# First layer of six experts as seven block products: a fused RWKV and top-1 expert kernel on one Trainium2 core

## The chip, the cores and the metric

The kernel runs on one core of a Trainium2 chip. The core has five engines with a queue of instructions each: TensorE (PE: matmuls; its weight loads are listed apart as PEld), VectorE (DVE), ScalarE (ACT), GpSimd (POOL) and SyncE (SP, which starts transfers here). They run side by side and meet only at semaphores; each takes its own instructions in order. TensorE writes to PSUM, which has eight banks of 512 fp32 numbers on each of 128 partitions; the other operands lie in SBUF. The metric is device time in microseconds for one execution; lower is better.

## The reference

All is fp32. Four sequences of 768 tokens with 8 heads of 48 go through a linear recurrence; its output, 3072 tokens of 384 numbers, goes to a layer of eight experts, of which each token visits the one with the highest logit:

```python
for t in range(S):
    cur = np.einsum('bhd,bhe->bhde', u[None] * kt, vt)
    y[:, :, t] = np.einsum('bhd,bhde->bhe', rt, state + cur)
    state = w[None, :, :, None] * state + np.einsum('bhd,bhe->bhde', kt, vt)
...
expert_idx = np.argmax(logits, axis=1)
gate_w = probs[np.arange(N), expert_idx]
for e in range(E):
    mask = expert_idx == e
    h = np.maximum(x[mask] @ w1[e], 0.0)      # 384 x 1024
    out[mask] = gate_w[mask, None] * (h @ w2[e])   # 1024 x 384
```

## The kernel before

**Order of the work.** Everything stands in an order written out by hand; each engine runs its part of that order, and waits between engines are put in where a tile is written and read (or written again). First comes the recurrence, 16 pairs of heads in chunks of 128 tokens (TensorE lines L276 to L349, with VectorE's scale L257, GpSimd's products L263 and L267, and `turn`, a GpSimd copy of one element, which holds GpSimd back until a certain tile is written). Each token's row is then written to a table in memory, sorted by expert. Two `early` passes take the first 160 tokens of experts 0 and 1. Then eight `late` passes follow, `k` = 0 to 7: 0 and 1 take the rest of experts 0 and 1, 2 to 7 take the other six experts by falling number of tokens. Their widths `n` are 224, 192, 416, 412, 408, 396, 380 and 364 columns (`WIDTH`, L35); a token is a column. A column beyond an expert's count is padding and isn't written out.

**A pass.** `load` brings the tokens (SP's queue), `xT` transposes them on VectorE (L457) into `t`, three tiles `m` of 128 numbers by `n` tokens. `L1` (L460) is the first layer: for each of eight tiles `f` of 128 hidden numbers, three matmuls over `m` into one of four banks (`hbank`, L70), and ScalarE's Relu (L468) out of the bank into `h`. The 1024 hidden numbers come in four quarters of two tiles, one weight tile `w1s[k % 2][q]` each. `L2` (L473) is the second layer for the columns beyond the first 256 (`c`): 24 products into three banks (`ybank`, L71), transposed back by VectorE (L482), weighted (L493) and scattered to the output by GpSimd (L499, L606). `tokens_out` (L501) is the second layer for the first 256 tokens of passes 2 to 7, in a 2x2x2 block form that is there already: two blocks of tokens, of hidden numbers and of output columns, seven products of blocks (L526) instead of eight. It needs sums of blocks of the weights (`weight_sums`, L579: eight operations on VectorE into `tums`) and of `h` (`inner_sums`, L594: four on VectorE into `sums`). VectorE and ScalarE combine its products (L544 to L559), and GpSimd scatters the rows of two blocks of 128 tokens (L573, L577).

**How the passes interleave** (L793 to L826). In pass `k` < 7 TensorE runs the first layer of pass `k` and then the second layer (`L2`, `tokens_out`) of pass `k - 1`, called `o`. Between the two, in VectorE's order, stand `o`'s sums and the transposes of pass `k + 1`. Then the loads of later weights and tokens are started. In the last stage `o`'s second layer comes ahead of pass 7's first layer, and pass 7's second layer ends the kernel. For `k` < 3 the output blocks of the early passes are scattered between the tiles of the first layer (L800 to L802).

**PSUM.** `X01[0]` and `X01[1]` are tiles of one bank. `X23` (L63) is one tile of two banks, used as `X23[:, 0, :]` and `X23[:, 1, :]`. `yps[0]`, `yps[1]`, `dsb` and `tr` are tiles of one bank each. The first layer uses the X banks, the second layer the others.

**A guard.** A flag counts conditions that the sorted form rests on; if one fails, a general program runs instead. One is a least number of tokens of each sorted expert (`lows`, L643).

Of the kernel before, what the change touches and what calls it, by code (L numbers as in the profile page):

```python
# [26 lines left out]
FT = F // 128  # L27
# [16 lines left out]
def straight(tc, rk, vk, w, w1, w2, out, flag):  # L44
# [26 lines left out]
    ybank = [yps[0], dsb, yps[1]]  # L71

# [357 lines left out]
    class Pass:  # L430
# [29 lines left out]
        def L1(self, fs=range(FT), then=()):  # L460

            h, then = self.h, list(then)
            for f in fs:
                p = hbank[f % 4]
                for m in range(DT):
                    nc.tensor.matmul(p[:, 0:self.n], lhsT=w1s[self.k % 2][f // 2][:, m, f % 2 * 128:(f % 2 + 1) * 128],  # L466
                                     rhs=self.t[:, m, 0:self.n], start=m == 0, stop=m == DT - 1, skip_group_check=True)
                nc.scalar.activation(h[:, f, 0:self.n], p[:, 0:self.n], func=ACT.Relu)  # L468
                if then:
                    load, k, q = then.pop(0)  # L470
                    load(k, (q,), nc.scalar)

        def L2(self):  # L473
# [3 lines left out]
            for m in range(DT):  # L477
                p = ybank[m]
# [22 lines left out]
        def tokens_out(self):  # L501
# [66 lines left out]
            product(dsb, 0, Sm(2), Tm(2))  # L568
            product(dsb, 1, Sm(3), B_(1, 1))
            add(so[6], dsb, 0, so[2])  # L570
            final(1, 1, dsb, 0, so[5])
            final(0, 1, dsb, 1, so[4])
            scatter(out, it2[:, 0:1], self.yt[0][:, :], N)  # L573
            weigh(so[7], so[6], 1)
            product(yps[1], 0, A(1, 1), Tm(3))
            final(1, 0, yps[1], 0, so[7])
            scatter(out, it2[:, 1:2], self.yt[1][:, :], N)  # L577

        def weight_sums(self):  # L579
# [5 lines left out]
            for q in range(2):  # L585
                o = slice(2 * q, 2 * q + 2)
                (b11, b12), (b21, b22) = [[halves(ws[q + u])[:, :, z] for z in range(2)] for u in (0, 2)]
                t1, t2, t3, t4 = [x[:, o].rearrange("p f (m c) -> p f m c", m=DT) for x in tums]
                op(t1, b12, b11, ALU.subtract)
                op(t2, b22, t1, ALU.subtract)  # L590
                op(t3, b22, b12, ALU.subtract)
                op(t4, b21, t2, ALU.subtract)

        def inner_sums(self):  # L594
# [5 lines left out]
            op(sums[0], a21, a22, ALU.add)  # L600
            op(sums[1], sums[0], a11, ALU.subtract)
            op(sums[2], a11, a21, ALU.subtract)
            op(sums[3], a12, sums[1], ALU.subtract)
# [11 lines left out]
    def op(o, a, b, how):  # L615
        nc.vector.tensor_tensor(o, a, b, op=how)
# [26 lines left out]
    nc.gpsimd.memset(lows[:, 2:], 256.0)  # L643
# [112 lines left out]
    so = [mp.tile([128, DM // 2], FP32, name=f"so{k}") for k in range(8)]  # L756
    vt, ia = [mp.tile([128, nt], I32, name=n) for n in ("vt", "ia")]
# [33 lines left out]
    waiting = [(x, j) for x in early for j in range(ge)]  # L791

    for k, p in enumerate(late):  # L793
        o = late[k - 1]
        if k < n - 1:

            for f in range(FT):
                p.L1((f,))
                if (k < 2 and f % 2 or k == 2 and f % 4 == 1) and waiting:
                    nc.gpsimd.tensor_copy(turn, p.h[0:1, f, 0:1])  # L800
                    x, j = waiting.pop(0)
                    x.blocks_out((j,))  # L802
            if k > 0:
                o.weight_sums()
                o.inner_sums()
            late[k + 1].xT()
            if k == 0:
                okay()
# [5 lines left out]
        else:  # L814
            o.weight_sums()
            o.inner_sums()
            o.L2()
            o.tokens_out()
            p.weight_sums()
            p.L1()  # L820
            weights1(p.k + 2)
            p.inner_sums()
# [519 lines left out]
```

## Time and profile before

| | |
|---|---|
| median of 9 runs | 386.67 us (384.38 to 389.01) |
| the profiled execution | 385.27 us |
| its span in the profile | 383.5 us |
| TensorE busy, matmuls | 367.9 us, 96% |
| VectorE, ScalarE, GpSimd busy | 48%, 35%, 40% |
| granted TensorE clock | 0.993 |
| first layer (L466), early and late | 384 + 96 matmul instructions |
| GpSimd's scatters of output (L606) | 57 |

The profile's page gives each engine's busy time, the chain of work that ended last (followed back from the last instruction to what released it each time), and groups of instructions: line, engine, operation, output from inputs, shape and number, then busy time and the mean duration of one, then the idle time in front of them and who ended it. The trace behind it can be asked for single instructions in order of time: start, duration, what. A product in fp32 is two matmul instructions for TensorE, so a first layer of 24 products is 48 instructions. Mean durations of matmuls overlap; what one adds to the row is read from how far apart they start, or from the chain.

### The profile page before, as it was taken

Reading aid. Unit: us, or ns where it says so; the run is one execution under the profiler, and the core shown is the slowest. Engines: PE = TensorE matmul, PEld = TensorE weight load, DVE = VectorE, ACT = ScalarE, POOL = GpSimd, SP = SyncE. Lnnn points to the kernel's source line nnn. Section 1 sums busy time; section 2 is a strip of 40 time slices with the busy share of each in tenths; the row PEclk is TensorE's granted clock in tenths of the full one; section 3 lists DMA queues with packets and bytes.
Section 4 is the critical chain, followed back from the end, with each engine's and each line's share of the span. In section 5 each row is a group of like instructions: output and inputs, shape, how many; then the busy total and the mean of one; then the engine's idle time right before and its main releaser. Section 6 shows DMA issues by size and latency. Waiting matters only on the chain.

```text
span 383.5 us, 8205 instructions
## 1 busy us (share of the span) xinstructions
PE 367.9 (96%) x3141; PEld 302.5 (79%) x3141; DVE 183.6 (48%) x437; ACT 133.4 (35%) x378; POOL 151.8 (40%) x176
## 2 busy tenths in 40 slices
PE   6999999999999999999999999999999999999990
PEld 6788888888877989995585599579669769996790
DVE  8977796895961224022115323702813722564331
ACT  2678787786773310310211202211220221112110
POOL 3379678888753420544113005105203402542042
PEclk9999999999999999999999999999999999999997
DMA  7998886867464883696728615823833833403301
GB/s 208 266 260 235 256 258 218 265 213 237 153 178 159 256 314 65 201 244 191 168 89 234 155 45 163 222 84 103 228 108 118 201 127 123 129 34 103 109 20 48
DMA packets 34977, 65.03 MB, mean 170 GB/s; under 512 B 18378, under 2 KB 19410, under 8 KB 34928
## 3 DMA queue, kind: packets, MB, share of 16 engines
q1 hardware_dynamic: 29392, 49.86, 46.7%
q0 software_dynamic: 3808, 9.84, 7.2%
q10 hardware_dynamic: 1728, 4.72, 3.6%
q8 instruction: 26, 0.43, 0.5%
q14 instruction: 23, 0.19, 0.1%
HBM read 53.29 MB, written 11.26 MB: 168 GB/s over the span
## 4 chain that ended last, share of the span: by engine, by line
PE 89%; issue 4%; POOL 2%; DVE 2%; ACT 1%; DMA 0%; DVEq 0%; ACTq 0%; POOLq 0%
PE X L466 33%; PE yps L480 10%; PE X L288 6%; PE yps L526 6%; PE yps L331 5%; PE dsb L480 5%; PE tr L526 4%; PE tr L349 4%; PE dsb L526 3%; PE yps L336 3%; PE tr L513 3%; PE dsb L311 2%; PE X L349 2%; PE dsb L276 2%; ACT A L294 1%
## 5 line engine op out<-in xcount | busy, mean ns | idle before, releaser
L466 PE MATMUL X<-xT,w1s 128*128 128x224 f32 (+7 forms) x384 | 113.9, 457 | 0.0
L466 PEld LDWEIGHTS X<-xT,w1s 128*128 128x128 f32 x384 | 71.4, 190 | 40.0 <-issue 21.2
L606 POOL DMA_INDIRECT out_dram<-yo,ix x33 | 32.3, 980 | 126.0 <-DVE ia L507 118.4
L468 ACT ACTIVATE hT<-X 128x224 f32<-128x224 f32 (+7 forms) x64 | 29.6, 462 | 118.4 <-PE X L466 101.9
L294 ACT ACTIVATE A<-ident,own 128x128 f32<-128x128 f32 x192 | 57.9, 388 | 8.2 <-DVE own L280 6.3
L401 POOL DMA_INDIRECT rows<-xb,slot x24 | 28.1, 1169 | 14.9 <-issue 10.1
L480 PEld LDWEIGHTS yps<-hT,w2s 128*128 128x128 f32 x256 | 32.5, 191 | 1.7 <-issue 0.9
L480 PE MATMUL yps<-hT,w2s 128*128 128x96 f32 (+7 forms) x256 | 33.3, 283 | 0.0
L288 PE MATMUL X<-RK 48*128 48x128 f32 x384 | 30.3, 289 | 1.8 <-DVE RK L257 1.8
L482 DVE STREAM_TRANSPOSE yq<-yps 128x160 f32<-128x160 f32 (+3 forms) x16 | 5.1, 318 | 52.5 <-PE yps L480 51.7
L288 PEld LDWEIGHTS X<-RK 48*128 48x128 f32 x384 | 24.0, 187 | 7.5 <-issue 4.3
L257 DVE TENSOR_TENSOR RK<-rk,TT 112x1536 f32<-112x1536 f32 x16 | 27.7, 1732 | 0.0
L263 POOL TENSOR_TENSOR rp<-rk 112x768 f32<-112x768 f32 x15 | 27.3, 1820 | 0.0
L300 DVE COPY_PREDICATED A<-strict,X 128x512 f32<-128x512 int32 x32 | 23.1, 738 | 4.5 <-ACT A L294 4.4
L331 PE MATMUL yps<-A,vk 128*48 128x128 f32 x384 | 24.3, 276 | 0.0
L606 POOL DMA_INDIRECT out_dram<-yt,it x14 | 15.4, 1101 | 20.8 <-ACT so L555 12.1
L331 PEld LDWEIGHTS yps<-A,vk 128*48 128x48 f32 x384 | 20.2, 123 | 1.9
L457 DVE STREAM_TRANSPOSE xT<-xs 128x416 f32<-128x416 f32 (+3 forms) x24 | 11.3, 521 | 20.8 <-DMA xs<-rows 20.8
L672 POOL COPY turn<-own 1x1 f32<-1x1 f32 x14 | 16.7, 1193 | 9.7 <-DVE own L280 9.2
L349 PE MATMUL tr<-sel,yT 112*128 112x104 f32 x128 | 18.6, 286 | 0.3 <-issue 0.3
L559 ACT COPY so<-tr 128x192 f32<-128x192 f32 x6 | 1.9, 320 | 48.2 <-PE tr L526 48.2
L349 PEld LDWEIGHTS tr<-sel,yT 112*128 112x128 f32 x128 | 15.7, 191 | 2.5 <-issue 0.4
(160 smaller groups left out, 529.3 us busy)
## 6 DMA issues: line engine op xcount, KB each, us to landing
w1s<-in_w_dram SPq DMA_DIRECT2D x36, 384.0 KB
rk<-in_rk_dram SPq DMA_DIRECT2D x16, 672.0 KB
w2s<-in_w_dram SPq DMA_DIRECT2D x24, 384.0 KB
vk<-in_vk_dram SPq DMA_DIRECT2D x16, 528.0 KB
w2s<-in_w_dram ACTq DMA_DIRECT2D x8, 384.0 KB
xs<-rows SPq DMA_DIRECT2D x16, 169.0 KB
w1s<-in_w_dram ACTq DMA_DIRECT2D x4, 384.0 KB
rows<-zt SPq DMA_DIRECT2D x1, 1248.0 KB
```

Of the source, the lines that this page charges most:

```text
L257: nc.vector.tensor_tensor(RKs[i % 3][0:KP].rearrange("p u (c t) -> p u c t", t=C), x[0:KP].rearrange("p u (c t) -> p u c t", t=C), bc(TT[: ...
L263: (eng or nc.gpsimd).tensor_tensor(rps[i % 2][0:KP], x[0:KP, 0], x[0:KP, 1], op=ALU.mult)
L288: nc.tensor.matmul(o, lhsT=r[q, 1, c * C:(c + 1) * C], rhs=r[q, 0, c * C:(c + 1) * C], start=True, stop=True, skip_group_check=True)
L294: nc.scalar.activation(A[:, place(c, h), :], ident, func=ACT.Copy, scale=own[i % 2][:, c, h:h + 1])
L331: nc.tensor.matmul(o(c, h), lhsT=v[:, c, h * D:(h + 1) * D], rhs=A[:, place(c, h), :], start=c < 2, stop=c == 0, skip_group_check=True)
L349: nc.tensor.matmul(trv[c // 4][:, c % 4, :], lhsT=yTs[i % 3][0:KP, c & 1, (c // 2) * C:(c // 2 + 1) * C], rhs=sel[:, c & 1, i % HP, :], st ...
L401: s_ = nc.gpsimd.indirect_dma_start(out=rows[:, :], out_offset=bass.IndirectOffsetOnAxis(ap=slot[b % 2][:, c:c + 1], axis=0), in_=xbs[b % ...
L466: nc.tensor.matmul(p[:, 0:self.n], lhsT=w1s[self.k % 2][f // 2][:, m, f % 2 * 128:(f % 2 + 1) * 128], rhs=self.t[:, m, 0:self.n], start=m ...
L468: nc.scalar.activation(h[:, f, 0:self.n], p[:, 0:self.n], func=ACT.Relu)
L480: nc.tensor.matmul(p[:, 0:n], lhsT=w2s[self.k % 2][f // 2][:, f % 2, m * 128:(m + 1) * 128], rhs=self.h[:, f, self.c:self.n], start=f == 0 ...
L526: nc.tensor.matmul(p[:, at * Z:(at + 1) * Z], lhsT=a(f), rhs=b(f), start=f == 0, stop=f == FT // 2 - 1, skip_group_check=True)
L606: s_ = nc.gpsimd.indirect_dma_start(out=to[:, :], out_offset=bass.IndirectOffsetOnAxis(ap=at, axis=0), in_=x, in_offset=None, bounds_check ...
```

## The change

The first layer of passes 2 to 7 takes the 2x2x2 block form as well, one quarter at a time (in pass 7 the first three quarters; the fourth stays as it was). The blocks are tiles `m` = 0 and 1, the two hidden tiles of the quarter, and two halves of the tokens; tile `m` = 2 is added to the same four outputs by plain products, one of them joined with another through `S[4]`. That makes 11 products of n/2 columns for 12 half products of each kind before. `quarter` gives their order and the banks: `pa` to `pd` are four banks, one set (`quads`) for quarters 0 and 2, the other for 1 and 3. VectorE and ScalarE combine the products into `h`.

The products need sums of weight blocks (`quarter_sums`: five VectorE operations of 128 by 128 a quarter, done a pass ahead) and of token blocks (`token_sums`: four of 128 by n/2 a pass). The late `L2` moves to the X banks (`zbank`). `weight_sums` of the second layer goes from VectorE to GpSimd. `inner_sums` is split into four, one behind each quarter. `tokens_out` computes its fifth and sixth product in the other order, in banks of their own, and issues its first scatter before the last two products. The guard's least number of tokens rises from 256 to 320.

```diff
+    zbank = hbank[0::2] + [X23[:, 0, :]]
+    quads = [zbank + [X23[:, 1, :]], [yps[0], dsb, yps[1], tr]]
...
+        def quarter(self, q):
+            n, w, t, sd = self.n // 2, w1s[self.k % 2][q], self.t, quart[q]
+            pa, pb, pc, pd = quads[q % 2]
+            def W(m, f):
+                return w[:, m, f * 128:(f + 1) * 128]
+            def T(m, z):
+                return t[:, m, z * n:(z + 1) * n]
+            def product(p, at, *ab):
+                for j, (a, b) in enumerate(ab):
+                    nc.tensor.matmul(p[:, at * n:(at + 1) * n], lhsT=a, rhs=b, start=j == 0, stop=j == len(ab) - 1,
+                                     skip_group_check=True)
+            def both(p):
+                return p[:, 0:2 * n].rearrange("p (z j) -> p z j", z=2)
+            S = [sd[:, j, :] for j in range(5)]
+            Y = [toks[j][:, 0:n] for j in range(4)]
+            a, u, v, x = mids[q % 2]
+            product(pa, 0, (W(0, 0), T(0, 0)))
+            product(pb, 0, (W(1, 0), T(1, 0)), (W(2, 0), T(2, 0)))
+            nc.scalar.copy(a[:, 0:n], pa[:, 0:n])
+            product(pb, 1, (S[1], Y[1]))
+            nc.vector.tensor_tensor(u[:, 0:2, 0:n], both(pb), bc(a[:, None, 0:n], [128, 2, n]), op=ALU.add)
+            product(pa, 1, (S[0], Y[0]), (W(2, 1), T(2, 1)))
+            nc.vector.tensor_tensor(v[:, 0:n], pa[:, n:2 * n], u[:, 1, 0:n], op=ALU.add)
+            product(pc, 1, (S[2], Y[2]))
+            product(pc, 0, (S[3], T(1, 1)), (S[4], T(2, 1)))
+            f = slice(2 * q, 2 * q + 2)
+            second = self.h[:, f, n:2 * n]
+            nc.vector.tensor_tensor(second, both(pc), bc(v[:, None, 0:n], [128, 2, n]), op=ALU.add)
+            nc.scalar.activation(second, second, func=ACT.Relu)
+            nc.vector.tensor_tensor(x[:, 0:n], pc[:, n:2 * n], u[:, 1, 0:n], op=ALU.add)
+            product(pd, 0, (W(1, 1), Y[3]), (W(2, 1), T(2, 0)))
+            nc.vector.tensor_tensor(u[:, 2, 0:n], pd[:, 0:n], x[:, 0:n], op=ALU.add)
+            nc.scalar.activation(self.h[:, f, 0:n], u[:, 0:3:2, 0:n], func=ACT.Relu)
+        def quarter_sums(self, q):
+            w, sd = w1s[self.k % 2][q], quart[q]
+            a11, a21 = [w[:, 0, f * 128:(f + 1) * 128] for f in range(2)]
+            a12, a22 = [w[:, 1, f * 128:(f + 1) * 128] for f in range(2)]
+            op(sd[:, 0, :], a21, a22, ALU.add)
+            op(sd[:, 1, :], sd[:, 0, :], a11, ALU.subtract)
+            op(sd[:, 2, :], a11, a21, ALU.subtract)
+            op(sd[:, 3, :], a12, sd[:, 1, :], ALU.subtract)
+            op(sd[:, 4, :], w[:, 2, 0:128], w[:, 2, 128:256], ALU.subtract)
+        def token_sums(self):
+            n = self.n // 2
+            b11, b12, b21, b22 = [self.t[:, m, z * n:(z + 1) * n] for m in range(2) for z in range(2)]
+            y = [toks[j][:, 0:n] for j in range(4)]
+            op(y[0], b12, b11, ALU.subtract)
...
-                p = ybank[m]
+                p = (zbank if self.nt else ybank)[m]
...
-            product(dsb, 0, Sm(2), Tm(2))
-            product(dsb, 1, Sm(3), B_(1, 1))
-            add(so[6], dsb, 0, so[2])
-            final(1, 1, dsb, 0, so[5])
-            final(0, 1, dsb, 1, so[4])
+            product(dsb, 0, Sm(3), B_(1, 1))
+            final(0, 1, dsb, 0, so[4])
             scatter(out, it2[:, 0:1], self.yt[0][:, :], N)
+            product(yps[1], 0, Sm(2), Tm(2))
+            add(so[6], yps[1], 0, so[2])
             weigh(so[7], so[6], 1)
-            product(yps[1], 0, A(1, 1), Tm(3))
-            final(1, 0, yps[1], 0, so[7])
+            final(1, 1, yps[1], 0, so[5])
+            product(tr, 0, A(1, 1), Tm(3))
+            final(1, 0, tr, 0, so[7])
...
-                op(t1, b12, b11, ALU.subtract)
+                op(t1, b12, b11, ALU.subtract, nc.gpsimd)
...
-    nc.gpsimd.memset(lows[:, 2:], 256.0)
+    nc.gpsimd.memset(lows[:, 2:], float(PAD))
...
+        if k == n - 1:
+            o.weight_sums()
+            o.inner_sums()
+            o.L2()
+            o.tokens_out()
+            p.weight_sums()
+            for q in range(3):
+                p.quarter(q)
+            p.L1(range(6, FT), bank=quads[1][2:] + quads[1][:2])
...
+                o.weight_sums()
+                for q in range(4):
+                    p.quarter(q)
+                    o.inner_sums((q,))
+                    if q > 1:
+                        late[k + 1].quarter_sums(q - 2)
...
             late[k + 1].xT()
+            if ahead:
+                late[k + 1].token_sums()
+                for q in range(0 if k == 1 else 2, 4 if k < n - 2 else 3):
+                    late[k + 1].quarter_sums(q)
```

## The prediction

> **What bounds the kernel now.** I read the page's first part, then the chain that ended last, then the groups of instructions by shape, then the order of single instructions on VectorE, ScalarE and GpSimd.
>
> ```profile
> PE 367.9 (96%) x3141; PEld 302.5 (79%) x3141; DVE 183.6 (48%) x437; ACT 133.4 (35%) x378; POOL 151.8 (40%) x176
> ```
>
> ```profile
> 178.23 16.76 PE X L466 x48
> 194.99 1.73 PE yps L480 x16
> ...
> 222.11 2.17 PE yps L480 x16
> 224.28 2.17 PE dsb L480 x16
> ...
> 228.63 2.60 PE tr L526 x16
> ...
> 300.89 15.32 PE X L466 x48
> ```
>
> From 149.9 us on, every piece of the chain is TensorE and each starts where the one before ends: TensorE has no gap in the expert part, so this part is as long as TensorE's instructions. Anything that shortens them shortens the kernel, and any wait put on TensorE lengthens it by its full length. The other engines are busy less than half the time; they matter only where TensorE is made to wait for them.
>
> ```profile
> L466 PE MATMUL X<-xT,w1s 128*128 128x416 f32 x48 | 16.9, 512 | 0.0
> ...
> L526 PE MATMUL dsb<-tums,sums 128*128 128x192 f32 x48 | 8.8, 326 | 0.0
> ...
> L616 DVE TENSOR_TENSOR tums<-w2s,w2s 128x384 f32<-128x384 f32 x12 | 6.6, 551 | 0.0
> ...
> L482 DVE STREAM_TRANSPOSE yq<-yps 128x160 f32<-128x160 f32 x8 | 2.8, 350 | 40.1 <-PE yps L480 40.1
> ...
> L263 POOL TENSOR_TENSOR rp<-rk 112x768 f32<-112x768 f32 x15 | 27.3, 1820 | 0.0
> ...
> L267 POOL TENSOR_TENSOR Kd<-vk,T 128x480 f32<-128x480 f32 x11 | 13.2, 1202 | 0.0
> ```
>
> Prices. By the chain, 48 matmul instructions (each fp32 product is two) of 416 columns take 16.76 us, 349.2 ns each, and 16 of 192 columns 2.60 us, 162.5 ns: 2.5 ns and 0.833 ns a column. VectorE's two-operand operation takes 152 ns and 1.04 ns an element (384: 0.55, 480: 0.65 us); one that needs nothing of its forerunner starts 0.08 us before that ends. GpSimd's takes 172 ns and 2.15 ns an element, so 1.0 us at 384.
>
> **Part 1: fewer columns.** A quarter had 12 instructions of n columns; it has 11 products of n/2, 22 instructions. A pass goes from 48 at n to 88 at n/2. For n = 416: 88 x 175.8 ns = 15.47 us for 16.76, 1.29 less; 412, 408, 396, 380: 1.27, 1.26, 1.22, 1.17 less. The last pass changes three quarters: 66 x 154.2 ns + 12 x 305.8 ns = 13.85 for 14.68, 0.83 less. Sum: **-7.04 us**, all on the path. That is sure: the rows of 192 columns run at that price in an unbroken row.
>
> **Part 2: the wait inside every even quarter.** The changed program's instruction order with its waits shows what the diff doesn't. In quarters 0 and 2 blocks pc and pd are the two halves of one tile, X23. The program keeps them apart as one tile: the first product of pd (toks3 into X23, second bank) waits for VectorE's `x` operation, which reads pc, the first bank. In quarters 1 and 3 the four blocks are four tiles, and that product waits for nothing. pd is the last block of a quarter, and TensorE takes its instructions in order, so the next quarter stands behind it. `x` itself comes after `second`, and `second` needs the last product of pc. So TensorE issues pc's last product, then stands idle for:
> - 0.16 us until that product is out (the group of L480 that starts at 221.94 ends at 224.28, and the next one starts at 224.12);
> - 0.04 until VectorE starts (224.28 to the transpose at 224.32);
> - `second`, 416 elements, 0.585 less 0.08: 0.50;
> - `x`, 208 elements: 0.37 (192: 0.36);
> - 0.05 back to TensorE (at the start of the attention, VectorE's L257 ends at 9.28 and TensorE's L288 starts at 9.33);
> - restart of TensorE, not shown apart in the trace: 0 (L288's weight load and matmul both start at 9.33) to 0.19 (one weight load); I take 0.05, nearest to that row.
>
> That is 1.17 us at n = 416 and 1.09 at 364, on average 1.14. There are two such quarters in each of six passes: 12 x 1.14 = **+13.7 us**. Bounds: without the first 0.16 (matmul ends are modelled) and the restart 12 x 0.93 = 11.2; with a full weight load each 15.4.
>
> **Part 3: the wait for the copy of pa.** The second half of pa likewise waits for ScalarE's copy `a` of its first half (same tile). That copy stands on ScalarE behind the Relu of the quarter before, which needs VectorE's last operation of that quarter. From the end of pd: 0.20 to VectorE, 0.37 for it, 0.05, Relu 0.52 less 0.10 overlap, copy 0.34 (192: 0.32), 0.05: 1.43 us. TensorE has four products in front, 1.41 us at n = 416 and 1.23 at 364. So quarters 1 and 3 wait 0.02 to 0.20, with the restart about 0.1, 11 times: 1.1. In front of quarter 2 the odd quarter's own `second` and `x` push VectorE's last operation back by 0.2: about 0.35, six times: 2.1. **+3.2 us**; bounds 0.5 (latencies a tenth shorter) and 6.
>
> **Part 4: weight sums on GpSimd.** Eight operations of 384 elements leave VectorE (0.55 each, 4.4 us a pass) and cost GpSimd 8.0 us. In passes 3 to 6 they stand behind the two token scatters of the pass before and end some 11 us into the pass; TensorE first reads them after its first layer, L480's products and the first two of L526, 23 us or more in: nothing, and the scatters queued behind them become ready only after that as well. In the last stage only the 5.4 us of L480 and two products of 1.30 stand between. GpSimd starts there some 2 us late (its scatters), six of the eight must be done, and the inner sums share its operands' way (below): ready at 9 to 10 us, wanted at 8.6: **+1.2 us**, bounds 0 and 4.
>
> **VectorE, queues, tail.** In the pass from 205.51 to 237.73 VectorE is busy 12.4 us. It gets 4 x 2.2 us of combining, 20 operations of 128 elements (0.23 apart, 4.6) and 4 of n/2 (1.4), and loses 4.4: near 23 us of a pass of 34. A quarter needs 2.2 us of it, with an inner sum (0.6) and the next pass's weight sums (1.15) 4.0, while TensorE takes 3.9 plus the waits; the two sets of four banks give a quarter's slack, so its load alone costs nothing. For pass 2 the transposed tokens (1.6), token sums (1.4) and weight sums (4.6) run from 167.11, where the tokens land, and with the second layer's transposes behind them end near 176.5; TensorE wants them at 178.23: 1.7 us spare. The loads on SP's queue wait for the same last readers as now, with a pass to land in: nothing. The tail: the first token scatter is ready two products earlier: -0.3.
>
> Sum against the profiled execution (385.27 us, span 383.5): -7.0 + 13.7 + 3.2 + 1.2 - 0.3 = +10.8, so 396.1. That execution lies 1.4 under the median of the runs, 386.67; from there **397.4 us**, 2.8% slower.
>
> **A rule weighed.** VectorE and GpSimd get in each other's way in this trace:
>
> ```profile
> 41.48 1.72 DVE L257 TENSOR_TENSOR RK<-rk,TT 112x1536 f32<-112x1536 f32 x1
> 41.69 1.55 POOL L672 COPY turn<-own 1x1 f32<-1x1 f32 x1 [1.28 <-DVE own L280]
> ...
> 62.96 2.12 POOL L672 COPY turn<-own 1x1 f32<-1x1 f32 x1 [0.36 <-issue]
> ...
> 15.75 1.19 POOL L267 TENSOR_TENSOR Kd<-vk,T 128x480 f32<-128x480 f32 x1
> 16.72 1.84 DVE L257 TENSOR_TENSOR RK<-rk,TT 112x1536 f32<-112x1536 f32 x1
> ```
>
> A copy of one element, 0.18 us elsewhere, takes 1.55 and ends when VectorE's L257 ends; the other way round L257 takes 1.84 instead of 1.72 where it starts inside a GpSimd operation. The Trainium skill, "SBUF — State Buffer", section "Who interferes with whom", says that a VectorE instruction with two SBUF inputs and a GpSimd instruction that reads SBUF exclude each other for a whole instruction. The rows agree, and it speaks against moving the weight sums: the inner sums (two SBUF inputs) now run beside them. By that rule, with turns taken, an inner sum waits for at most one GpSimd operation, which the quarter's slack holds, and the sum stays at 397.4; without any exclusion the last stage would wait 0.3 instead of 1.2 and the sum be 396.5.
>
> **The rivals.**
> 1. *GpSimd keeps the way for its whole run.* The copy at 62.96 (2.12 us) waits out two VectorE operations that follow each other without a gap, so a run may hold on. Then the inner sum after quarter 0 waits up to four operations, and with it VectorE, ScalarE's copy and quarter 2: some 1.3 us in each of passes 3 to 6: +5.5, 402.9. Against it: four of eight operations wait for the one before, which leaves gaps.
> 2. *The waits cost their lower bounds:* -7.3 + 11.2 + 0.5 = +4.4, 391.1.
> 3. *Other side: the wait for `x` is met before TensorE arrives,* and the saved columns remain: 386.67 - 7.0 - 0.3 + 1.2 = 380.6. It decides once the idle time of an even quarter is under 7.3 / 12 = 0.6 us. `second` and `x` alone stream 624 elements, 0.65 us at 1.04 ns. Hardly.
> 4. *The change does not do what it says.* The order has 88 matmul instructions for 48 and the sums on GpSimd; only the price could differ. Busy time over count gives 8.8 / 48 = 183 ns for 192 columns; at that price 88 of 208 columns (196 ns) take 17.3 us against 16.76 and the columns cost 2.9 us instead of saving 7.0: 407. But each group's busy time holds the 0.16 us in which it overlaps the next, and the chain's 162.5 ns doesn't.
>
> **Chances.** Forecast 0.68, rival 1 0.20, rival 2 0.07, rival 3 and any other gain 0.05. The range, 391.5 to 404, takes in both ends of the waits and rival 1; the forecast's own is 393 to 401. About 0.5% can be told from no change here: faster 0.05, same 0.03, slower 0.92.
>
> **What would show it.** In the changed profile: matmul groups of 208 columns near 15.4 us of issue a pass; idle time of TensorE before the X23 products of the first layer, released by VectorE's `x` line, 12 times near 1.1 us, and none before those of tr; short idle times before pa's second half, released by ScalarE's copy; one wait for GpSimd in the last stage; a TensorE share below 96%. No idle time before X23 would make the forecast wrong; idle times of several microseconds released by the copy in passes 3 to 6 would be rival 1.

## The result, and the profile after

The changed kernel takes **409.0 us** (median of 10 runs, 407.4 to 412.2) against 387.29 for the kernel before beside it: 1.0565 times as long, 95% interval 1.0531 to 1.0598. The forecast of 397.4 had the sign and half of the size, and the time lies outside its range. The profiled execution has a span of 406.4 us (383.5 before).

The experiments ran in five more sessions on five chips, and the six sessions fell into two kinds. The kernel before takes 385 to 387 us in the one and 381 in the other; the changed kernel tells them apart much more clearly:

| | before, us | changed, us | ratio (95%) |
|---|---|---|---|
| first comparison | 387.29 | 409.0 | 1.0565 (1.0531 to 1.0598) |
| again, in another session | 385.83 | 407.25 | 1.0551 (1.0485 to 1.0616) |
| again, in a third one | 380.82 | 393.38 | 1.0311 (1.0279 to 1.0343) |

I call the chip of the first two "late" (the reason comes below; whether it was one chip or two isn't known) and that of the third "prompt". On the prompt one the change costs 12.6 us, near the 10.7 forecast; on the late ones some 9 us more. Since each of the five chips was met in one session only, "chip" here and below can also mean the occasion.

The page's first part, of the changed kernel on a late chip and then on the prompt one:

```profile
PE 371.1 (91%) x3371; PEld 336.1 (83%) x3371; DVE 244.8 (60%) x643; ACT 140.2 (34%) x401; POOL 201.7 (50%) x224
```

```profile
PE 366.2 (93%) x3371; PEld 333.8 (85%) x3371; DVE 246.5 (63%) x643; ACT 140.3 (36%) x401; POOL 201.9 (52%) x224
```

TensorE's share fell from 96% by waits. They are these: TensorE's waits from 150 us on (line, what it waited for, us in total, times, longest), late chip, then prompt chip (from 140 us):

```profile
PE X L490 <- DVE midx L512: 11.7, 12, 1.3
PE X L490 <- ACT mida L501: 6.3, 9, 1.7
PE yps L591 <- POOL tums L680: 2.4, 1, 2.4
```

```profile
PE X L490 <- DVE midx L512: 11.2, 12, 1.0
PE X L490 <- ACT mida L501: 1.0, 5, 0.2
PE yps L591 <- POOL tums L680: 0.6, 1, 0.6
```

The first row is the wait for `x`, twelve times, as forecast, on both kinds. The second and third rows differ by 5.3 and 1.8 us. The view counts idle time from the end of the matmul before, which otherwise overlaps the next one by 0.16 us, so each wait costs 0.16 us more than it says. The first matmul behind a wait costs another 0.10 us (0.28 from its start to the next one, where 0.17 to 0.18 is usual), and waits under some 0.15 us are not in the view.

Where it lies, in lengths of the first layer (from its first matmul to the next layer's first) and of the stretch of second layers ahead of pass 7:

| us | pass 2 | 3 | 4 | 5 | 6 | 7 | last stage's second layers |
|---|---|---|---|---|---|---|---|
| before (both profiles, late chips) | 16.8 | 16.6 | 16.4 | 16.0 | 15.3 | 14.7 | 29.3 to 29.5 |
| changed, prompt chip | 18.8 | 18.6 | 18.4 | 17.9 | 17.3 | 16.9 | 30.2 |
| changed, late chip (first) | 18.9 | 18.6 | 20.2 | 19.9 | 19.3 | 17.9 | 33.6 |

The kernel before was not profiled on a prompt chip. Of the 14.6 us between the two spans of the changed kernel 4.4 lie ahead of pass 2 (it starts at 178.28 us and at 173.91); the kernel before takes 4 to 7 us longer on the late chips as well. The rest of the late chip's surplus sits at passes 4 to 7 and in the last stage. The start of pass 4, TensorE's order (start, us, what, and in brackets the idle time before and who ended it), late chip:

```profile
242.00 1.20 PE L490 MATMUL X<-xT,w1s 128*128 128x204 f32 x6
243.04 0.51 PE L490 MATMUL X<-toks,quart 128*128 128x204 f32 x2
245.06 0.61 PE L490 MATMUL X<-toks,quart 128*128 128x204 f32 x2 [1.51 <-ACT mida L501]
...
246.20 0.85 PE L490 MATMUL X<-xT,quart 128*128 128x204 f32 x4
248.00 0.61 PE L490 MATMUL X<-toks,w1s 128*128 128x204 f32 x2 [0.95 <-DVE midx L512]
```

and the prompt one:

```profile
237.47 1.20 PE L490 MATMUL X<-xT,w1s 128*128 128x204 f32 x6
238.51 0.85 PE L490 MATMUL X<-toks,quart 128*128 128x204 f32 x4
...
239.89 0.85 PE L490 MATMUL X<-xT,quart 128*128 128x204 f32 x4
241.69 0.61 PE L490 MATMUL X<-toks,w1s 128*128 128x204 f32 x2 [0.95 <-DVE midx L512]
```

The last line of both is the forecast wait. The 1.51 us before it, for ScalarE's copy `a`, is on the late chip alone. There VectorE's last operation of `tokens_out` and ScalarE's copy start together, long after the products that they read. VectorE, then ScalarE, late chip:

```profile
241.24 0.41 DVE L616 SCALAR_TENSOR_TENSOR yt<-yps,xg,so 128x192 f32<-128x192 f32 x1
244.65 0.42 DVE L616 SCALAR_TENSOR_TENSOR yt<-tr,xg,so 128x192 f32<-128x192 f32 x1 [3.00 <-PE X L490]
```

```profile
244.68 0.33 ACT L501 COPY mida<-X 128x204 f32<-128x204 f32 x1 [2.87 <-PE X L490]
```

The trace's records have the last four products that step TensorE's semaphore (two into `tr`, two into X banks) out at 241.52, 242.17, 242.51 and 243.55. The recorded steps come at 244.49, 244.56, 244.60 and 244.68: four in 0.19 us, while the products themselves end 0.34 to 1.04 us apart. So the products were done and their semaphore steps 1.1 to 3.0 us late. On the prompt chip the same four steps come 0.02 us or less behind the recorded ends, and the copy starts at 238.08, 0.1 us after its product is out. Passes 5 and 6 and the last stage show the same on the first two late chips.

In the last stage it does more harm. GpSimd's scatters and first weight sum there, late chip, then prompt chip:

```profile
346.78 0.98 POOL L670 DMA_INDIRECT out_dram<-yt,it  x1 [0.30 <-DVE so L609]
349.76 1.17 POOL L670 DMA_INDIRECT out_dram<-yt,it  x1 [2.00 <-DVE yt L616]
350.94 1.02 POOL L680 TENSOR_TENSOR tums<-w2s 128x384 f32<-128x384 f32 x1
```

```profile
336.52 0.98 POOL L670 DMA_INDIRECT out_dram<-yt,it  x1 [0.30 <-DVE yt L616]
337.80 1.09 POOL L670 DMA_INDIRECT out_dram<-yt,it  x1 [0.30 <-DMA w2s<-in_w_dram]
338.89 1.03 POOL L680 TENSOR_TENSOR tums<-w2s 128x384 f32<-128x384 f32 x1
```

The second token scatter waits 2 us for VectorE's last `final`, which waited for the late semaphore, and the weight sums queue behind it. TensorE then waits for them, late chip:

```profile
354.97 0.81 PE L591 MATMUL yps<-tums,sums 128*128 128x192 f32 x4
358.20 3.23 PE L591 MATMUL yps<-tums,sums 128*128 128x192 f32 x12 [2.42 <-POOL tums L680]
```

and pays once more. Stretches of that time (window, its length, busy time of PE, PEld, DVE, ACT and POOL, granted TensorE clock, share of the DMA engines, GB/s):

```profile
355.50:358.20 2.70, 0.28 (x2) 0.00 (x1) 2.67 (x7) 0.04 (x1) 2.62 (x4) 1.00 0.00 0
358.20:359.20 1.00, 1.00 (x6) 1.00 (x7) 0.23 (x1) 0.45 (x1) 1.00 (x2) 1.00 0.00 0
359.30:362.50 3.20, 3.20 (x11) 3.20 (x11) 0.72 (x2) 0.18 (x1) 2.72 (x3) 0.50 0.04 15
```

A microsecond after the wait the clock is 0.50 for the whole of a 3.2 us window, in which 11 matmuls take the time of 20. By the trace's clock record it is 0.50 for 3.41 us, from 359.24; half of that is 1.7 us. The prompt chip's wait of 0.6 us is followed by no such stretch. So 1.8 us more of wait became 3.4 us more of stage (33.6 against 30.2).

### The profile page after: what moved, and what is told of

Read it like the earlier page. It is cut to its first block, busy times and chain, and to the rows that moved or that the text cites. A ratio compares the mean times of both kernels' runs of the same rounds, so it can differ in the third digit from the quotient of the medians.

```text
span 406.4 us, 9048 instructions
## 1 busy us (share of the span) xinstructions
PE 371.1 (91%) x3371; PEld 336.1 (83%) x3371; DVE 244.8 (60%) x643; ACT 140.2 (34%) x401; POOL 201.7 (50%) x224
## 4 chain that ended last, share of the span: by engine, by line
PE 81%; DVE 6%; issue 5%; POOL 3%; ACT 2%; POOLq 0%; DVEq 0%; ACTq 0%
PE X L490 11%; PE X L545 10%; PE X L468 8%; PE yps L490 6%; PE X L290 6%; PE yps L591 6%; PE yps L333 5%; PE tr L591 5%; PE tr L351 4%; PE yps L338 3%; PE dsb L490 3%; PE tr L578 3%; DVE hT L510 2%; PE yps L545 2%; PE dsb L591 2%
## 5 line engine op out<-in xcount | busy, mean ns | idle before, releaser
L545 PE MATMUL X<-hT,w2s 128*128 128x96 f32 (+7 forms) x384 | 47.4, 283 | 0.0
L545 PEld LDWEIGHTS X<-hT,w2s 128*128 128x128 f32 x384 | 47.2, 191 | 0.2
L511 ACT ACTIVATE hT<-hT 128x416 f32<-128x416 f32 (+5 forms) x23 | 12.3, 534 | 62.2 <-DVE hT L510 62.2
L591 PE MATMUL yps<-tums,sums 128*128 128x192 f32 x144 | 26.6, 336 | 2.4 <-POOL tums L680 2.4
L680 POOL TENSOR_TENSOR tums<-w2s,tums 128x384 f32<-128x384 f32 x24 | 26.6, 1109 | 0.9
L591 PEld LDWEIGHTS yps<-tums,sums 128*128 128x128 f32 x144 | 24.5, 195 | 2.7 <-POOL tums L680 2.7
L490 PE MATMUL X<-xT,w1s 128*128 128x208 f32 (+5 forms) x120 | 26.0, 331 | 0.0
L490 PE MATMUL X<-toks,quart 128*128 128x208 f32 (+5 forms) x72 | 18.6, 345 | 6.5 <-ACT mida L501 6.3
L333 PEld LDWEIGHTS yps<-A,vk 128*48 128x48 f32 x384 | 20.2, 123 | 1.9
L490 PEld LDWEIGHTS X<-xT,w1s 128*128 128x128 f32 x120 | 20.9, 190 | 0.5
L670 POOL DMA_INDIRECT out_dram<-yt,it x14 | 13.9, 992 | 14.6 <-DMA xs<-rows 6.5
L490 PEld LDWEIGHTS X<-toks,quart 128*128 128x128 f32 x72 | 12.2, 189 | 9.5 <-ACT mida L501 9.5
```

What stands on the lines that cost most here:

```text
L333: nc.tensor.matmul(o(c, h), lhsT=v[:, c, h * D:(h + 1) * D], rhs=A[:, place(c, h), :], start=c < 2, stop=c == 0, skip_group_check=True)
L490: nc.tensor.matmul(p[:, at * n:(at + 1) * n], lhsT=a, rhs=b, start=j == 0, stop=j == len(ab) - 1, skip_group_check=True)
L545: nc.tensor.matmul(p[:, 0:n], lhsT=w2s[self.k % 2][f // 2][:, f % 2, m * 128:(m + 1) * 128], rhs=self.h[:, f, self.c:self.n], start=f == 0 ...
L591: nc.tensor.matmul(p[:, at * Z:(at + 1) * Z], lhsT=a(f), rhs=b(f), start=f == 0, stop=f == FT // 2 - 1, skip_group_check=True)
L670: s_ = nc.gpsimd.indirect_dma_start(out=to[:, :], out_offset=bass.IndirectOffsetOnAxis(ap=at, axis=0), in_=x, in_offset=None, bounds_check ...
L680: (eng or nc.vector).tensor_tensor(o, a, b, op=how)
```

## The experiments

**Other pairs of banks.** No set of four banks holds both halves of X23 any more.

```diff
-    quads = [zbank + [X23[:, 1, :]], [yps[0], dsb, yps[1], tr]]
+    quads = [zbank + [tr], [yps[0], dsb, yps[1], X23[:, 1, :]]]
```

> The even quarters take tr as their fourth bank and the odd ones X23's second bank, so that no quarter has both banks of the tile X23. Theory 1 (the product into X23's second bank waits for VectorE's reading of the first one, because both banks are one tile): in the changed kernel's trace the 12 even quarters each have one gap of 1.2 to 1.6 us between two products there where 0.17 is usual, 14.7 us with the slow restart behind each; all 12 go, some of it comes back because ScalarE's copy in the odd quarters then comes later for TensorE (up to 0.3 us in 11 quarters): 396 to 398.5 us against the changed kernel's 409.0, ratio to the kernel before about 1.025. Rival (the sums that VectorE has to do are what is late, whatever the bank): the wait moves to the next product that needs VectorE or to the copy, less than 6 us are gained, 403 or more.

381.59 us; ratio 1.0016 (0.9982 to 1.0049), on a chip where the kernel before took 381.35. Against the changed kernel on the prompt chip (1.0311) this is 11.2 us by the ratios, the expected gain; the expected time was counted from the late chip's 409 and so too high. TensorE's waits:

```profile
PE yps L490 <- ACT mida L501: 2.2, 11, 0.2
PE X L490 <- ACT mida L501: 1.0, 5, 0.2
PE yps L591 <- POOL tums L680: 0.6, 1, 0.6
```

All twelve waits for `x` are gone, and, as expected, the odd quarters now wait 0.2 us for the copy (2.2 us in place of under 0.15 each). One line of bank assignment is worth the whole loss on a prompt chip; VectorE's load was not the cause.

**Three suspects for the late semaphores.** The first puts the token and quarter sums behind the second layer's transposes on VectorE (in the changed kernel they stand ahead of them, and the scatters of `yo` follow). The second delays the loads of the next tokens. The third takes the last stage's weight sums back to VectorE.

```diff
-            if ahead:
-                late[k + 1].token_sums()
-                for q in range(0 if k == 1 else 2, 4 if k < n - 2 else 3):
-                    late[k + 1].quarter_sums(q)
...
                 o.L2()
+                if ahead:
+                    late[k + 1].token_sums()
+                    for q in range(0 if k == 1 else 2, 4 if k < n - 2 else 3):
+                        late[k + 1].quarter_sums(q)
                 o.tokens_out()
```

> The token sums and the sums of quarters 2 and 3 of the next pass stand behind the second layer's transposes on VectorE instead of ahead of them. In the changed kernel's trace VectorE is busy without a break from 226.9 to 236.0 us, the second layer's transposes of pass 3 run at 233.88 and its first scatter starts at 235.87, 9.3 us into that layer, where the kernel before has it 5.7 us into it; the scatters then run into the loads of the next pass's rows, and at the start of passes 4, 5 and 6 TensorE's semaphore reaches ScalarE and VectorE some 2 us late and the copy that the fourth product waits for is late with it (1.85 to 2.03 us from one product to the next, where 0.17 is usual). Theory A (the late scatters make a pile of transfers, and the pile holds up the semaphores): the scatters start about 3.5 us earlier, the three gaps and the smaller one of the last stage shrink to 0.3 or less, 4 to 6 us are gained: 403 to 405 us, ratio about 1.043. Theory B (the load of the next rows alone does it, or the first token scatter at that place): the gaps stay, 408 to 410 us.

```diff
                     p.quarter(q)
+                    if q == 0 and k + 1 < n and k > 2:
+                        nc.scalar.copy(late[k + 1].x[0:1, 0, 0:1], p.h[0:1, 0, 0:1])
+                    if q == 0 and k > 2:
+                        late[k + 1].load()
...
-        if k + 2 < n:
+        if k + 2 < n and k < 2:
             late[k + 2].load()
```

> The loads of the sorted rows of passes 4 to 7 wait for the first quarter of the pass before (by one element that ScalarE writes into their tile behind that quarter), so none of them is under way while a pass starts; the scatters stay where they are. Theory A (a pile of scatters and loads holds up the semaphores): the gaps of 1.85 to 2.03 us at the starts of passes 4, 5 and 6 shrink to under 0.5, 3 to 5 us gained, 404 to 406 us. Theory B (the scatters alone do it): the gaps stay, 408 to 410 us. If the load comes too late for the transposes of its pass, a new wait of TensorE for them would be seen at the end of passes 3 to 6, and the time would rise.

```diff
-        def weight_sums(self):
+        def weight_sums(self, eng=nc.gpsimd):
...
-            o.weight_sums()
+            o.weight_sums(nc.vector)
             o.inner_sums()
             o.L2()
```

> Only the weight sums of the second layer at the head of the last stage go back from GpSimd to VectorE. In the changed kernel that stage is 4.2 us longer than before, with one wait of TensorE of 2.42 us for these sums, which start at 350.94 us on GpSimd behind a token scatter. Theory (GpSimd starts them late and runs them at 1.3 to 1.4 us each beside VectorE's sums): the wait goes, and the stage is as long as before or up to 1 us longer: 405 to 406 us, ratio about 1.047. Rival (the stage is long for what comes ahead of it, the late semaphore at 349 us): under 2.5 us gained, 407 us or more.

Measured, all with the kernel before at 381.35: 393.81 us (1.0331, 1.0294 to 1.0367), 393.9 (1.0337, 1.03 to 1.0375) and 392.19 (1.0295, 1.0258 to 1.0332). None of the three profiles has a wide gap at a pass start, and the third edit touches nothing there. That pointed to the chip, and the comparison told nothing of the suspects. The last one did show its own part: the last stage went from 30.2 to 29.3 us, the length that it has in the kernel before. VectorE's inner sums there, changed kernel on the late chip, then this variant (on the prompt chip the changed kernel's longest one takes 1.80 us too):

```profile
350.11 0.69 DVE L680 TENSOR_TENSOR sums<-sums,hT 128x512 f32<-128x512 f32 x1
350.72 1.80 DVE L680 TENSOR_TENSOR sums<-hT 128x512 f32<-128x512 f32 x1
```

```profile
341.52 0.69 DVE L680 TENSOR_TENSOR sums<-sums,hT 128x512 f32<-128x512 f32 x1
342.13 0.68 DVE L680 TENSOR_TENSOR sums<-hT 128x512 f32<-128x512 f32 x1
```

An inner sum that starts beside GpSimd's weight sums takes 1.80 us instead of 0.68: it waits out about one GpSimd operation (1.0 us), as a turn taken would have it.

**The changed kernel again, twice, and the kernel before.**

> The changed kernel as it is, again. In the three runs that keep the shared bank (sums behind the second layer, later loads, weight sums of the last stage on VectorE) the wide gaps at the starts of passes 4 to 6 were gone in all three, in the third one too, where nothing near them was changed; the kernel before itself took 381.35 us there against 387.29. Theory 1 (the late semaphores at the pass starts belong to the chip or the occasion, not to the program): on a chip that shows 381 us for the kernel before, the gaps are absent here too, 393 to 394.5 us, ratio about 1.032. Theory 2 (each of the three edits removes them by itself): the gaps of about 1.9 us stand at the starts of passes 4 to 6, 399 us or more, ratio 1.047 or more.

> The kernel before, profiled beside the changed one on the same chip. Theory 1 (chip or occasion): the stretches of the second layer and of the ordinary first layer are as long as in its first profile within 0.1 us (16.8, 16.6, 16.4, 16.0, 15.3 and 14.7 us for the first layers of passes 2 to 7), and what it is faster by, some 6 us, lies ahead of pass 2. Theory 2: the passes themselves are shorter here.

407.25 us, 1.0551, with the gaps (waits of 1.4 to 1.6 us for the copy at the starts of passes 4 to 6). The chip was of the late kind, so this could not decide. The kernel before took 383.81 us there in one run, and its passes have the lengths of its first profile within 0.1 us. Both are late chips, so this says nothing of the two kinds; its TensorE has no wait from 140 us on in either profile.

> The changed kernel a third time. If the kernel before takes 381 us: by the theory that the late semaphores go with the chip no wide gap at a pass start, 393 to 394.5 us, ratio 1.032 to 1.036; by the theory that each of the edits took them away itself 399 us or more. If the kernel before takes 384 us or more: as twice before, gaps of 1.8 to 2.0 us, ratio about 1.055.

393.38 us, 1.0311 (1.0279 to 1.0343), no gaps. The late semaphores go with the chip or the session; the program is the same in all three.

**The suspects on a late chip.** Two more tries on prompt chips told nothing, as they said beforehand:

> The sums behind the second layer, once more, because the wide gaps at the pass starts stood in both profiles of the changed kernel where the kernel before took 386 to 387 us, and in none of the four variants where it took 381 us. If the kernel before takes 384 us or more here: theory A (scatters that come 3.5 us later than before make a pile of transfers, and TensorE's semaphores are held up behind it) has the gaps of 1.8 to 2.0 us at the starts of passes 4, 5 and 6 under 0.5, 396 to 402 us; theory B (the load of the next rows does it by itself, or the chip alone) has the gaps as they are, 405 to 408 us. If the kernel before takes 381 us, no gaps, and nothing is told apart.

> The later loads of the rows, once more, for the same reason. If the kernel before takes 384 us or more: theory A has the gaps under 0.5 us here as well, because the pile needs scatters and loads together, 396 to 402 us; a theory C (the scatters alone hold up the semaphores) has them as they are, 405 to 408 us. If the kernel before takes 381 us, no gaps, and nothing is told apart.

> The sums behind the second layer. Kernel before at 384 us or more: theory A (late scatters make the pile) 396 to 402 us and gaps under 0.5 us at the starts of passes 4 to 6; theory B (the loads or the chip alone) 405 to 408 us with the gaps. Kernel before at 381 us: 393.8 us as twice before.

393.72 (1.0351), 393.94 (1.0345) and 394.11 us (1.033). The last session met a late chip (kernel before 384.91):

> The sums behind the second layer. Kernel before at 384 us or more: theory A (late scatters make the pile) 396 to 402 us with gaps under 0.5 us at the starts of passes 4 to 6; theory B (the loads of the next rows, or the chip alone) 405 to 408 us with the gaps. Kernel before at 381 us: 394 us, nothing told apart.

> The later loads of rows. Kernel before at 384 us or more: theory A and theory B (the loads are needed for it) 396 to 402 us, gaps under 0.5 us; theory C (the scatters alone) 405 to 408 us. Kernel before at 381 us: 394 us, nothing told apart.

406.68 us (1.057, 1.0499 to 1.0642) and 407.69 (1.0605, 1.0564 to 1.0646). TensorE at the start of pass 4, first with the sums behind the second layer, then with the later loads:

```profile
242.13 0.51 PE L490 MATMUL X<-toks,quart 128*128 128x204 f32 x2
243.37 0.61 PE L490 MATMUL X<-toks,quart 128*128 128x204 f32 x2 [0.73 <-ACT mida L501]
```

```profile
241.45 0.51 PE L490 MATMUL X<-toks,quart 128*128 128x204 f32 x2
243.33 0.61 PE L490 MATMUL X<-toks,quart 128*128 128x204 f32 x2 [1.37 <-ACT mida L501]
```

The loads have nothing to do with it: the DMA engines' share from 236 to 244 us fell to 0.44 (0.83 from 238 to 246 in the changed kernel), the first load of rows was issued at 248.52, and the gap stayed. So the loads are not needed for it, and 407.69 us lies where theory C, the scatters alone, had it. Earlier scatters halve the wait (0.7 to 0.9 us in place of 1.4 to 1.7), but pass 2 takes 0.4 us more and the last stage keeps its 33.7 us; 406.68 us missed theory A's 396 to 402, and the ratio (1.057 for 1.055 and 1.0565) shows no gain. The expectation had also misread the kernel before: its second layer ahead of pass 4 starts at 221.9 us and its first scatter at 230.20, 8.3 us into it, not 5.7. The changed kernel has 9.5 (226.38 to 235.87) and this one 8.3, so the change had put the scatters back by 1.2 us only, and this edit takes back all of it. GpSimd's first scatter of `yo` and its first token scatter in this run:

```profile
233.73 0.99 POOL L670 DMA_INDIRECT out_dram<-yo,ix  x1 [16.41 <-DVE toks L680]
...
240.28 0.98 POOL L670 DMA_INDIRECT out_dram<-yt,it  x1 [0.30 <-issue]
```

What the late profiles of these three kernels share at the starts of passes 4 to 6: the held steps of TensorE's semaphore come 1.95 to 2.25 us after the first token scatter starts (once, in pass 6 with the sums behind the second layer, 1.4). 240.28 to 242.23 here, 240.70 to 242.83 with the later loads, 242.31 to 244.49, 278.14 to 280.39 and 313.33 to 315.53 in the changed kernel. Move the scatter, and the release moves with it; move the loads, and it stays.

The records of the steps show how general this is. Take each instruction that steps a semaphore of its engine and ask whether a step is recorded within 0.13 us of its end. On the prompt chip all 402 of TensorE's in the changed kernel are. In its first profile 74 of the 402 are not (and 24 of VectorE's 526, 29 of ScalarE's 398): the step comes later or is missing from the record. None of these ends before the kernel's first scatter (54.77 us), and of TensorE's 74, 72 end within 2.3 us of the start of a scatter, where 155 of the 402 lie in all. The kernel before has the same on its late chips, 52 of 318 in its first profile. So it is not TensorE alone that is late and not the passes alone, and the change did not make the lateness: it made TensorE wait for it.

That GpSimd's scatters are what holds the steps up is the best reading of this. No run left the scatters out, why some chips do it and others don't is open, and whether the recording has a part in it (steps are missing on late chips alone) isn't shown.

**Taking the copy out of the way.** Other pairs, and pa's second half behind the products into the third bank, so that the copy has three products' time more.

```diff
-            product(pa, 1, (S[0], Y[0]), (W(2, 1), T(2, 1)))
-            nc.vector.tensor_tensor(v[:, 0:n], pa[:, n:2 * n], u[:, 1, 0:n], op=ALU.add)
             product(pc, 1, (S[2], Y[2]))
             product(pc, 0, (S[3], T(1, 1)), (S[4], T(2, 1)))
+            product(pa, 1, (S[0], Y[0]), (W(2, 1), T(2, 1)))
+            nc.vector.tensor_tensor(v[:, 0:n], pa[:, n:2 * n], u[:, 1, 0:n], op=ALU.add)
```

> As the run with other pairs of banks, and the fourth product of a quarter (the second half of its first bank) behind the products into the third bank, so that ScalarE's copy has three products' time more. Theory (what is left of waits inside quarters is the fourth product's wait for the copy, which reads the other half of the same bank: in the run with other pairs 0.48 to 0.54 us in place of 0.17 at quarters 1, 2 and 3 of a pass, with 0.11 of restart, 1.4 us a pass): these waits go, 7 to 8 us gained on 381.6: 373.5 to 375 us, ratio about 0.981. Rival (VectorE's sums come later with the fourth product, and the wait moves to a bank or to the next quarter's copy): under 3 us gained, 378.5 or more.

> As the run before it, with the weight sums of the second layer at the head of the last stage on VectorE as well. They gave 0.9 us of that stage (30.2 to 29.3 us) when nothing else was changed: 372.5 to 374 us, ratio about 0.979; no difference to the run before it if that stage's wait comes back in another place.

In the session of that second late result: 387.09 us (1.0027, 0.9983 to 1.0071) and 384.6 (0.996, 0.9918 to 1.0003), 20 and 23 us under the changed kernel on the same chip, but not the expected 0.981. The waits inside quarters are gone (first layers of passes 2 and 3: 15.6 and 15.3 us). What is left in the first of them lies where the late chips have it in the changed kernel: passes 4 to 6 take 16.3 to 16.6 us, with a wait of 1.0 to 2.1 us at each start, and the last stage 34.3 with a wait of 3.1 us for the weight sums.

**All edits together**: the last kernel with the sums behind the second layer, and the same with the later loads.

> All edits that took away a wait, together: other pairs of banks, the fourth product behind the third bank's, the last stage's weight sums on VectorE, and the token and quarter sums behind the second layer. Without late semaphores: the kernel before less the 7 us of columns, less up to 1, plus 0.5 to 1.5 us of what VectorE does later: ratio 0.980 to 0.985. With late semaphores (the kernel before at 384 or more): by theory A the same ratio, since the scatters come early again; by theory B that of the run without the last edit, 0.996.

> The run before it, with the loads of passes 4 to 7 behind the first quarter of the pass before as well. By theory A no further gain, or up to 1 us: ratio 0.978 to 0.985 on either kind of chip. By theory B (the load of the rows holds up the semaphores) 3 to 6 us less than the run before it where the kernel before takes 384 or more.

373.12 us, ratio 0.9794 (0.9754 to 0.9835), with the kernel before at 380.5, and 375.93, 0.9847 (0.9794 to 0.99): the later loads bring nothing. The passes of the second are as long within 0.1 us; its profile is longer ahead of pass 2, where the clock was 0.50 from 11.6 to 18.4 us. The first was run on two more chips:

> All edits together. Kernel before at 381 us: ratio 0.979 as before. Kernel before at 384 us or more: theory A the same ratio, 0.978 to 0.985; theory B that of the same kernel with the sums ahead of the second layer, 0.996.

> All edits together. Kernel before at 384 us or more: theory A a ratio of 0.978 to 0.985, theory B 0.996. Kernel before at 381 us: 0.979 to 0.984 as twice before.

375.61, 0.9836 (0.9793 to 0.9878), on a prompt chip, and 379.89, 0.9876 (0.9838 to 0.9913), on a late one. It beats both kernels on both kinds, the kernel before by 1.2 to 2.1%. The chain that ended last, by engine, on a prompt chip:

```profile
PE 93%; DMA 3%; POOL 1%; DVE 1%; SPq 0%; ACT 0%; issue 0%; POOLq 0%; DVEq 0%
```

TensorE has no wait from 140 us on there. On the late chip one is left, in pass 7:

```profile
PE yps L490 <- ACT mida L501: 1.5, 1, 1.5
```

There the token scatter still starts 2.02 to 2.05 us ahead of the late semaphores, but 0.8 us ahead of the pass instead of 0.3 to 0.5 behind its start, and three more products stand in front of the one that needs the copy: the lateness is covered. What the bank pairs and the order of products give apart from each other on a late chip, no run shows.

## Why the prediction was wrong, step by step

| step | forecast | prompt chip | late chip (first) |
|---|---|---|---|
| columns | -7.0 | -6.7 | -6.7 |
| wait for `x` | +13.7 | +14.4 | +14.9 |
| wait for the copy | +3.2 | +4.8 | +11.3 |
| last stage | +1.2 | +0.7 | +4.2 |
| tail | -0.3 | -0.5 | -0.7 |
| sum | +10.8 | +12.7 | +23.0 |

The columns are read from the kernel with all edits on a prompt chip, where passes 2 to 7 have no wait above 0.15 us left: 89.1 us against 95.8. The waits are the surplus of each step between matmuls over the usual one. All is counted against the first profile of the kernel before; against its second one, last stage and tail of the prompt chip are +0.9 and -0.9. The measured spans differ by 22.9 us on the late chip, the medians by 12.6 on the prompt one.

*Part 1 was right:* 88 matmuls at half width cost what the rows of 192 columns said. Rival 4 (183 ns) is out.

*Part 2 was right in place, number and size:* 12 waits of about 1.2 us with the restart, for the reason given, as the bank experiment shows. The 0.05 us taken for the restart was too low; it is 0.10, inside the bounds of 0 and 0.19.

*Part 3 is the step that failed.* "TensorE has four products in front" of the copy was reckoned for quarters 1 to 3, and there it was a little low: 0.2 us in quarters 1 and 3, 0.4 to 0.5 in quarter 2, 4.8 in all, because the restart comes on top each time. Quarter 0 was given no wait at all. The text gives no reason for that nothing; what it counts for the others, the Relu of the quarter before on ScalarE, quarter 0 doesn't have in front of its copy. On the late chips quarter 0 waits 1.4 to 1.7 us at the starts of passes 4 to 6, and with pass 7's that costs 6.4 us in the first profile. The trace of before could not show it as a wait: the Relu of a whole tile that stood there before is wanted only four tiles later. Its own profiles from late chips do have semaphore steps of TensorE a microsecond and more behind their products just ahead of passes 4 and 5 (at 237.41 and 269.29 us in the first, 2.07 and 2.06 us after the start of the last scatter of `yo`), and they cost nothing there. I had priced a path from TensorE to ScalarE and back by its usual delay and not asked how much slack it has just where the scatters run.

*Part 4:* in passes 3 to 6 the weight sums on GpSimd cost nothing, as said. In the last stage +1.2 was near on the prompt chip (0.7 to 0.9). The text's own terms, 5.4 us and two products of 1.30, put the sums' being wanted at 8.0 us, not at 8.6; in both profiles TensorE came to them 8.8 us into that second layer (347.01 to 355.78 on the late chip). On the late one the same lateness came through a chain that the text had half of (GpSimd's scatters ahead of the sums) and met the clock.

*What was named as hidden and wasn't looked at:* the token and quarter sums stand on VectorE ahead of the second layer's transposes, so the scatters start 9.5 us into that layer instead of 8.3. I had counted VectorE's load against the pass and not what queues behind it; by the lengths of passes 4 to 6 in the experiment this is worth 0.8 us a pass on a late chip and nothing on a prompt one.

*The rivals:* 1 did not occur (four passes at its 1.3 us would have been 5.2, not 5.5). Inner sums beside GpSimd stretch, but by one operation at a time (1.80 us at most), and TensorE doesn't notice. The rule of the Trainium skill ("SBUF — State Buffer", "Who interferes with whom") gave the right picture there: two inputs in SBUF against GpSimd's reads, taken in turns. 2 and 3 are out by the twelve waits. The mechanism that made the other 10 us was in no rival.

## What to carry to other kernels

Ask of every new product which tile its bank belongs to: two halves of one tile wait for each other's readers, and choosing the pairs otherwise gave back 11 us here. When a change shortens the time between a product and the next one that needs its result to go through another engine, look for slack where scatters and loads are thick; a path that is short of it turns a chip's small differences into full waits. Measure on more than one chip: the same program was 3.1% or 5.5 to 5.7% slower.

## What was not expected of the hardware

- In three of the six sessions TensorE's semaphore steps came 1 to 3 us late and in a bunch at the starts of passes 4 to 6 (four steps within 0.19 us, at 244.49 to 244.68), released about 2.1 us after a GpSimd scatter's start; in the others the copy started 0.1 us after its product was out. VectorE's and ScalarE's steps are held near scatters as well. Throughput doesn't tell the chips apart: behind the first 120 us a packet of 3072 bytes took 155 ns on average on the first chip and 156 on a prompt one.
- A TensorE wait of 2.42 us was followed, a microsecond after its end, by a granted clock of 0.50 for 3.41 us; waits of 2.35 to 2.44 us in the three other late profiles with the same bank pairs brought the mean clock of the 13 us around them down to 0.87. With other pairs a wait of 3.06 us was followed by the same 3.41 us, and one of 2.05 us in the same profile by no drop; nor were those of 1.51 to 1.89 us. The Trainium skill, "TensorE: Matmul & The Clock Gate", section "HAM oscillation — how this bites in real kernels", puts the rule at idle gaps above about 3.4 us; here 2.4 us were enough.
